# Experts: the order of all engines' steps given as a list, in place of a greedy planner

## The chip, the cores and the metric

The kernel runs on one core of a Trainium2 chip. The metric is the device time of one execution in microseconds. Five engines take their instructions in order, each from its own stream, and wait for each other through semaphores: TensorE (PE, with weight loads as PEld), VectorE (DVE), ScalarE (ACT), GpSimd (POOL) and SyncE (SP, which issues DMAs). The three timed runs of the kernel before took 904.2, 904.42 and 906.09 us.

## The reference

Attention comes first: 8 batches, 8 heads, 576 tokens of 64 numbers each, causal softmax joined with a linear memory `M_prev` by a gate from `beta`. Its output, 4608 tokens of 512 numbers, goes to 8 experts:

```python
logits = x @ w_gate                       # 4608 x 8
order = np.argsort(-logits.flatten())     # token-expert pairs, best first
# a token takes the first expert that still has room (576 tokens each)
h = np.maximum(x[mask] @ w1[e], 0.0)      # 512 -> 1024
out[mask] = h @ w2[e]                     # 1024 -> 512
```

The sort is never made. Expert by expert, the kernel finds the logit at which the fullest expert reaches 576 tokens, assigns these tokens, takes them out and goes on.

## The kernel before, in words

The attention part (lines up to 1413) and its own planner's numbers (`PR`) are the same before and after. The change is in the experts' part, `moe_all`, and it concerns order alone.

`moe_all` builds a list of steps. `SC.add(name, [(engine, duration)], function, r=, w=, after=, acq=, rel=, prio=)` adds one; `r` and `w` name what it reads and writes, from which its predecessors follow; `acq` and `rel` take and free a buffer of a pool (`pr` 2, `ph` 2, `py` 2 banks of PSUM, `ys` 3, `wst` 4 in SBUF). `SC.run` (line 763) then orders all steps: it goes through planned time, and for each engine takes, of the steps that could start within `tol` of the earliest, the one with the smallest `prio`. `prio` comes from `PM`, a table of offsets by kind of step and by expert. The durations in the code are the planner's. At last `for x in ...: x.fn(x)` issues each step's instructions in that order, so that the list is the order on every engine. Semaphores are set by the framework from what instructions really read and write; a wrong belief of the planner costs time, not correctness.

For each of eight experts (n = 0 to 7) there are these groups of steps:

- **Routing** (n < 7): six DVE steps prepare the logits, PE turns them, DVE copies them to `LwT`. Twelve rounds of bisection follow. In a round ACT (`sign`, L1656) and DVE (two counts, L1658) count how many logits pass three thresholds; DVE prepares the next base (`bs`, L1659); a matmul (L1417 `pr<-c,blk`) sums the counts over partitions; DVE compares (`kk`, L1664) and sets the next threshold (`th`, L1665). Then come `lo`, `hi`, the choice of the expert, ties and its tokens.
- **Lists**: prefix sums and comparisons (`triF`, `X`, `se`, `sa`, `oh`, counts, `ids`) give the 576 token numbers in five pieces. POOL gathers each (L1496), and the tokens are turned by a DMA, for n = 0 by PE (L1533) with copies by DVE and ACT (L1538, L1539).
- **Weights**: SP reads the expert's number into a register and issues four loads of 1 MB into `wst` (k = 0, 1 are w1, 2, 3 are w2). Each is split into two float16 parts in two halves: ACT scales in place (L1572) and copies to `wh` (L1573), POOL subtracts to `wl` (L1574, step `sp`, numbered 0 to 7). For the first two halves of n = 0 ACT does both (L1569) and DVE subtracts (L1570, `sv`).
- **FFN** (PE, two products of 192 and 112 matmuls, L1417): first product, for each of 8 f, 12 pairs of matmuls into `ph` and `prem`; ACT takes ReLU (`hh`, L1616), DVE the low part (`hl`, L1617), which frees `ph`. Second product, row tiles i = 0, 4, 1, 2, 3 of 24 or 16 matmuls into `py`; ACT takes it to `ys` (L1631; for i = 4 with DVE, L1633 and L1634), POOL scatters it (L1636). For n = 0 the first two f run tile by tile (`first`), as the tokens arrive.

While PE is in the FFN of expert n, DVE, ACT and POOL route expert n + 2 at most, gather its tokens and split its weights, and the routing matmuls of twelve rounds stand between those of the FFN.

The staging buffer `wst` was freed for the planner with the second half's subtraction (`rel=[('wst',B)] if h==1`).

Of the kernel before, what the change touches and what calls it, by code (L numbers as in the profile page):

```python
# [722 lines left out]
PM = {'T0': -3424.04,  # L723
 'TE': -702.39,
 'dl': {'0': {'gather': -1836.58, 'hh': -28.8, 'hl': 3481.83, 'list': 2655.0, 'moe': -21.88, 'route': -449.74, 'scat': 628.6, 'split': 797.73, 'turn': 806.47, 'wload': -1061.14},
        '1': {'gather': -2182.93, 'hh': -561.25, 'hl': -507.97, 'list': 738.65, 'moe': -816.64, 'route': 1812.2, 'scat': 1447.48, 'split': -1917.9, 'turn': 1120.92, 'wload': 569.59},
        '2': {'gather': 803.19, 'hh': -3791.98, 'hl': -2517.75, 'list': 4060.27, 'moe': -2830.38, 'route': 1411.82, 'scat': -257.8, 'split': -767.47, 'turn': -699.12, 'wload': -520.47},
        '3': {'gather': 783.42, 'hh': 752.55, 'hl': -4377.08, 'list': 117.47, 'moe': 2959.38, 'route': 123.24, 'scat': 1084.4, 'split': -825.2, 'turn': 559.13, 'wload': -4384.5},
        '4': {'gather': 645.39, 'hh': 463.84, 'hl': -2065.23, 'list': 314.59, 'moe': -2361.69, 'route': 677.63, 'scat': -3330.92, 'split': 4348.68, 'turn': 4693.11, 'wload': 723.19},
        '5': {'gather': 1141.95, 'hh': -1781.07, 'hl': -1655.72, 'list': 1577.46, 'moe': -593.59, 'route': 1224.57, 'scat': 232.55, 'split': 2059.93, 'turn': 2978.05, 'wload': 2114.96},  # L730
        '6': {'gather': -1842.39, 'hh': -359.44, 'hl': 2014.66, 'list': -966.97, 'moe': -1531.6, 'route': -1010.83, 'scat': 39.14, 'split': -3339.22, 'turn': -4662.8, 'wload': -443.47},
        '7': {'gather': -755.49, 'hh': 1071.48, 'hl': -182.98, 'list': 1302.37, 'moe': 2877.95, 'route': -1338.67, 'scat': -1147.04, 'split': 1130.89, 'turn': 1140.99, 'wload': 1242.07}},
 'off': {'gather': -603.49, 'hh': -1284.7, 'hl': -3245.18, 'list': -2019.85, 'moe': 3320.21, 'route': -4237.96, 'scat': -1349.2, 'split': 1057.19, 'turn': -14.46, 'wload': 519.8},
 'ph': 2000.0,
 'run': {'tol': 26.8},
 's0': 2}
# [7 lines left out]
class Sched:  # L744
# [18 lines left out]
    def run(self,tol=100,sem=170,same=110,t0=0.0,hwg=450,dlat=1300,dend=950,ph=2800.0,thr=3060,pel=60):  # L763
# [650 lines left out]
def moe_all(ctx,tc,Lw,cst,xd,w1,w2,out):  # L1414
# [3 lines left out]
    P_=PM  # L1418
# [33 lines left out]
    def pr(nm,n,x=0.0):  # L1452
        return P_['T0']+P_['TE']*n+P_['off'].get(nm,0.0)+x+DL.get(str(n),{}).get(nm,0.0)
# [24 lines left out]
    def lists(n):  # L1478
# [49 lines left out]
        if n==0:  # L1528
            for i in range(5):
# [5 lines left out]
                a=SC.add('turn',[('T',430)],f,r=[('xg',i)],acq=(pn,),prio=pr('turn',0),wg=1024)  # L1535
# [10 lines left out]
    def weights(n,ks=(0,1,2,3)):  # L1546
# [4 lines left out]
        for k in ks:  # L1551
# [11 lines left out]
            fl=lambda t: t.rearrange('p a b -> p (a b)')  # L1563
            for h in range(2):
                s=slice(2*h,2*h+2); ws=lambda B=B,s=s: wst[B.buf['wst']][:,s]
                pc=k*2+h; key=('w',n%2,k,h)
                rel=[('wst',B)] if h==1 else ()
                if n==0 and pc<P_.get('s0',4) or [n,pc] in P_.get('sv',[]):
                    a=SC.add('sa1',[('A',947)],lambda x,ws=ws,k=k,s=s: A_.activation(wh[:,k,s],ws(),AF.Copy,scale=64.0),w=[key+('h',)],after=[ld],prio=pr('split',n,.5*pc))  # L1569
                    SC.add('sv',[('V',1135)],lambda x,ws=ws,k=k,s=s: V_.scalar_tensor_tensor(fl(wl[:,k,s]),fl(ws()),64.0,fl(wh[:,k,s]),op0=ALU.mult,op1=ALU.subtract),r=[key+('h',)],w=[key+('l',)],after=[ld],rel=rel,prio=pr('split',n,.5*pc))  # L1570
                else:
                    a=SC.add('sa2',[('A',947)],lambda x,ws=ws: A_.activation(ws(),ws(),AF.Copy,scale=64.0),after=[ld],prio=pr('split',n,.5*pc))  # L1572
                    b=SC.add('sa3',[('A',947)],lambda x,ws=ws,k=k,s=s: A_.copy(wh[:,k,s],ws()),w=[key+('h',)],after=[a],prio=pr('split',n,.5*pc))  # L1573
                    SC.add('sp',[('P',2079)],lambda x,ws=ws,k=k,s=s: G_.tensor_sub(wl[:,k,s],ws(),wh[:,k,s]),r=[key+('h',)],w=[key+('l',)],after=[b],rel=rel,prio=pr('split',n,.5*pc))  # L1574
# [4 lines left out]
    def ffn(n):  # L1579
# [23 lines left out]
        for f in range(8):  # L1603
# [16 lines left out]
        for i in (0,4,1,2,3):  # L1620
# [15 lines left out]
            SC.add('scat',[('P',1250 if i<4 else 1200,'p',0,(1250,'n'))],lambda x,e=e,i=i,r_=r_: G_.indirect_dma_start(out=outv[5*n+i],out_offset=bass.IndirectOffsetOnAxis(ap=idx[0:r_,i:i+1],axis=0),in_=yss[e.buf['ys']][0:r_],in_offset=None),r=[('idx',n%3,i)],after=[e],rel=[('ys',e)],prio=pr('scat',n,pos[0]))  # L1636
    for n in range(8):
        if n<7:
# [14 lines left out]
            for r in range(NR):  # L1653
                i=r%2; t_,b_,c_=th[i],bs[i],cc[i]; x0=rp['x']
                for j in range(KV,K_):
                    SC.add('sign',[('A',547)],lambda x,j=j,t_=t_,c_=c_: A_.activation(scs[j-KV],LwT,AF.Sign,bias=t_[:,4:5],accum_out=c_[:,j:j+1]),r=['LwT',('th',i)],w=[('c',i,j)],prio=pr('route',n,rp['x']))  # L1656
# [72 lines left out]
    for x in SC.run(ph=P_.get('ph',5000.0),**P_.get('run',{})): x.fn(x)  # L1729
# [45 lines left out]
```

## Time and profile before

| | us |
|---|---|
| median of three timed runs | 904.42 |
| the profiled execution | 910.64 |
| its span, first to last instruction | 908.8 |
| PE busy | 803.3 (88%) |
| DVE busy | 670.7 (74%) |
| ACT busy | 580.7 (64%) |
| POOL busy | 543.7 (60%) |

The profile is of one execution. A matmul's end is modelled, so the busy time of PE is more than its work; from start to start is the better measure of it. Times on POOL are rough. A row of the timeline gives the start, the length, engine, line, operation, output and inputs, and in brackets how long the engine was idle before and what ended that. All times are from the span's start. Attention lasts until about 434 us, then PE waits for the routing of expert 0; its first FFN matmul is at 484.4 us and the last one of expert 7 at about 899.4.

### The profile page before, as it was taken

To read this page: it belongs to the slowest core of one execution; us is meant where nothing else is said; L and a number is where in the kernel's file an instruction comes from. 1 tells how busy PE (TensorE), PEld (TensorE's weight loads), DVE (VectorE), ACT (ScalarE), POOL (GpSimd) and SP (SyncE) were. 2 spreads that over 40 slices of the span, in tenths; PEclk is the share of its full clock that TensorE was granted. 3 is DMA by queue.
4 is the path that set the end of the run, shared out by engine and by line. 5 is a ranking of instruction groups with operands and counts; after the bars stand their busy time and mean duration, and the time that the engine had idled before them with its cause. 6 is when DMAs were issued, how large, how long until landed. Compare 5 with 4: busy or idle time off the path is not lost.

```text
span 908.8 us, 24389 instructions
## 1 busy us (share of the span) xinstructions
PE 803.3 (88%) x9240; PEld 526.2 (58%) x9240; DVE 670.7 (74%) x2507; ACT 580.7 (64%) x1027; POOL 543.7 (60%) x564
## 2 busy tenths in 40 slices
PE   3687998999999899999226999999999999999995
PEld 2475887777787688888115445454444444444442
DVE  8798898999999899997788878787867774111020
ACT  4767787887898888976226674848383846552120
POOL 5776886887898786866104492928174646852101
PEclk9999899999999999999557999999999999999998
DMA  5566777765757566334124455566463828940001
GB/s 127 117 142 132 166 155 156 165 149 127 161 130 168 120 139 136 86 71 92 48 93 146 164 144 195 143 213 148 167 168 124 226 89 208 248 150 18 35 13 41
DMA packets 231755, 120.86 MB, mean 133 GB/s; under 512 B 199509, under 2 KB 208725, under 8 KB 231637
## 3 DMA queue, kind: packets, MB, share of 16 engines
q1 hardware_dynamic: 225749, 100.42, 45.2%
q0 software_dynamic: 5888, 18.88, 6.7%
q8 instruction: 72, 1.18, 0.5%
q14 instruction: 46, 0.38, 0.1%
HBM read 72.40 MB, written 18.87 MB: 100 GB/s over the span
## 4 chain that ended last, share of the span: by engine, by line
PE 49%; DVE 22%; issue 12%; DMA 6%; POOL 5%; ACT 3%; SPq 2%; another core or an unknown queue 0%; POOLq 0%; DVEq 0%; ACTq 0%
PE py L1417 15%; PE ph L1417 15%; PE pb L892 7%; PE avo L892 5%; DVE pb L1067 4%; DVE scr L1658 2%; DVE xt L1264 2%; DMA xT<-xs 2%; PE pb L1052 2%; PE prem L1417 2%; DVE pl L1210 2%; SPq L959 1%; POOL h L1043 1%; PE pr L1417 1%; DMA qM<-qT 1%
## 5 line engine op out<-in xcount | busy, mean ns | idle before, releaser
L1574 POOL TENSOR_TENSOR wl<-wst,wh 128x1024 f16<-128x1024 f32 x62 | 131.3, 2140 | 80.8 <-ACT wh L1573 59.5
L1417 PE MATMUL ph<-xT,wh 128*128 128x512 f16 (+1 forms) x560 | 162.9, 364 | 2.8 <-DVE hl L1617 1.4
L1067 DVE CUSTOM_DVE_ANT_0 pb<-pb,maskF 128x128 f32<-128x128 f32 (+3 forms) x256 | 124.7, 497 | 7.4 <-PE pb L892 3.7
L892 PE MATMUL pb<-qT,kT 128*128 128x64 f16 (+3 forms) x576 | 106.1, 245 | 8.2 <-DVE mx L1067 1.8
L1636 POOL DMA_INDIRECT out_dram<-ys,idx x40 | 38.9, 973 | 119.1 <-ACT ys L1631 99.8
L1205 ACT ACTIVATE ph<-pb 128x512 f16<-128x512 f32 x144 | 86.0, 597 | 29.1 <-PE pb L892 23.0
L1617 DVE SCALAR_TENSOR_TENSOR hl<-ph,hh 128x512 f16<-128x512 f32 x64 | 44.0, 688 | 80.2 <-ACT hh L1616 77.2
L1417 PEld LDWEIGHTS <-wh 128*128 128x128 f16 x1072 | 68.4, 98 | 59.6 <-issue 3.5
L892 PE MATMUL pb<-qM,kB 128*128 128x64 f16 (+3 forms) x576 | 99.2, 244 | 1.7 <-DMA qM<-mr 1.7
L1417 PE MATMUL py<-wh,hh 128*128 128x512 f16 x256 | 97.0, 379 | 1.5 <-ACT hh L1616 1.1
L1417 PE MATMUL ph<-xT,wl 128*128 128x512 f16 (+1 forms) x280 | 97.7, 363 | 0.0
L1417 PE MATMUL py<-wl,hh 128*128 128x512 f16 x256 | 97.0, 379 | 0.0
L1417 PE MATMUL prem<-xT,wh 128*128 128x64 f16 x512 | 96.3, 193 | 0.0
L1658 DVE TENSOR_SCALAR_CACHE_REDUCE scr<-p_LwT,th 128x320 f16<-128x320 f32 x168 | 85.1, 543 | 2.7
L1616 ACT ACTIVATE hh<-ph 128x512 f16<-128x512 f32 x64 | 38.0, 593 | 76.2 <-PE ph L1417 55.5
L892 PE MATMUL pb<-kT,qM 128*128 128x512 f16 (+5 forms) x384 | 77.6, 314 | 8.8 <-DVE mx L1067 3.4
L1417 PEld LDWEIGHTS <-hh 128*128 128x128 f16 x512 | 47.3, 97 | 56.2 <-ACT hh L1616 1.3
L1656 ACT ACTIVATE scs<-p_LwT,th 128x320 f16<-128x320 f32 x84 | 47.0, 560 | 50.7 <-DVE th L1665 40.2
L892 PE MATMUL avo<-V,ph 128*128 128x65 f16 x1344 | 78.7, 194 | 0.0
L892 PE MATMUL avo<-V,pl 128*128 128x65 f16 x672 | 74.9, 196 | 0.0
L892 PEld LDWEIGHTS <-ph 128*128 128x128 f16 x1344 | 70.6, 98 | 5.1 <-issue 0.9
L1496 POOL DMA_INDIRECT xg<-xd,idx x40 | 38.6, 964 | 51.6 <-DVE sa L1517 35.0
(304 smaller groups left out, 2358.3 us busy)
## 6 DMA issues: line engine op xcount, KB each, us to landing
wst<-in_moe_w_dram SPq DMA_DIRECT2D x32, 1024.0 KB, 7.7
kf<-in_k_dram SPq DMA_DIRECT2D x64, 128.0 KB, 2.8
qf<-in_q_dram SPq DMA_DIRECT2D x64, 128.0 KB, 2.8
xd<-xs SPq DMA_DIRECT2D x16, 512.0 KB, 3.5
vf<-in_v_dram SPq DMA_DIRECT2D x48, 128.0 KB, 2.8
kB<-kT SPq DMA_DIRECT2D x15, 288.0 KB, 3.4
qM<-qT SPq DMA_DIRECT2D x15, 288.0 KB, 5.5
vF<-in_v_dram SPq DMA_DIRECT2D x16, 128.0 KB, 3.1
```

What stands on the lines that cost most here:

```text
L892: def MM(*a,**kw): mm(*a,skip_group_check=True,**kw)
L1052: for i in range(a,b_): nc.tensor.transpose(p[:,128*(i-a):128*(i-a)+128],g()[:,i],cst['idh'])
L1067: Q=lambda o,i,n: nc.vector.tensor_tensor_reduce(out=i,in0=i,in1=cst['maskF'][:,512-n:512],scale=1.0,scalar=-3e38,op0=ALU.add,op1=ALU.max, ...
L1205: c=SC.add('Eh',[('A',478)],lambda x,a=a: nc.scalar.activation(phs_[x.buf['ph']][:,0:512],pbb[a.buf['pb']],AF.Exp,scale=0.125),acq=('ph',) ...
L1417: def MM(*a,**kw): mm(*a,skip_group_check=True,**kw)
L1496: SC.add('gather',[('P',1250 if i<4 else 1200,'p',0,(1250,'n'))],lambda x: G_.indirect_dma_start(out=xg[0:r_,i],out_offset=None,in_=xd,in_ ...
L1574: SC.add('sp',[('P',2079)],lambda x,ws=ws,k=k,s=s: G_.tensor_sub(wl[:,k,s],ws(),wh[:,k,s]),r=[key+('h',)],w=[key+('l',)],after=[b],rel=rel ...
L1616: b=SC.add('hh',[('A',478)],lambda x,a0=a0,f=f: A_.activation(hh[:,f],phb[a0.buf['ph']],AF.Relu),w=[('hh',f)],after=[y],prio=pr('hh',n,pos ...
L1617: SC.add('hl',[('V',602)],lambda x,a0=a0,f=f: V_.scalar_tensor_tensor(hl[:,f],phb[a0.buf['ph']],0.0,hh[:,f],op0=ALU.max,op1=ALU.subtract), ...
L1636: SC.add('scat',[('P',1250 if i<4 else 1200,'p',0,(1250,'n'))],lambda x,e=e,i=i,r_=r_: G_.indirect_dma_start(out=outv[5*n+i],out_offset=ba ...
L1656: SC.add('sign',[('A',547)],lambda x,j=j,t_=t_,c_=c_: A_.activation(scs[j-KV],LwT,AF.Sign,bias=t_[:,4:5],accum_out=c_[:,j:j+1]),r=['LwT',( ...
L1658: V(462,lambda x,j=j,t_=t_,c_=c_: V_.tensor_scalar(scr[j],LwT,t_[:,j+1:j+2],0.0,op0=ALU.is_ge,op1=ALU.add,accum_out=c_[:,j:j+1]),r=['LwT', ...
```

## The change

`SC.run` gets an argument: with `order` it doesn't plan but calls the new `given`, which walks a list of step numbers, checks that each step's predecessors are ahead of it, and hands out the buffers that a third string names. `PM` loses its offsets. Many durations change, which now order nothing. A new step `wrel` of no engine frees `wst` after both halves' last readers.

```diff
-PM = {'T0': -3424.04, ... 'run': {'tol': 26.8}, 's0': 2}
+PM = {'T0': -3424.04, 'TE': -702.39, 'dl': {}, 'off': {}, 'ph': 2000.0, 's0': 2}
+PM_ORDER = ('''
+0 1 2 3 4 5 8 7 9 6 11 12 10 13 16 14 15 17 18 19 20 23 21 22 25 26 24 27 29 28 ...
+''','''
+
+''','''
+010101010021103010100111200011310210011010013020100112001102011301200110011100120 ...
+''')
...
+    def given(self,ids,alts,bufs):
+        al,bu=[iter(''.join(x.split())) for x in (alts,bufs)]; free={k:set(range(v)) for k,v in self.pools.items()}; out=[]
+        for i in map(int,ids.split()):
+            x=self.n[i]; a=x.alts[int(next(al)) if len(x.alts)>1 else 0]; x.eng=a[0]; x.var=a[2] if len(a)>2 else None
+            assert all(d.start is not None for d in x.deps)
+            for p in x.acq: x.buf[p]=int(next(bu)); free[p].remove(x.buf[p])
+            for p,o in x.rel: free[p].add(o.buf[p])
+            x.start=len(out); out.append(x)
+        assert len(out)==len(self.n)
+        return out
+    def run(self,order=None,tol=100,...):
+        if order: return self.given(*order)
...
# gather 1250 or 1200 -> 965 or 930; turn 430 -> 600; sp 2079 -> 2100; M 243 -> 245;
# hh 478 -> 490; scat 1250 or 1200 -> 980 or 905; sign 547 -> 465
...
-                rel=[('wst',B)] if h==1 else ()
+                both.append(z)
+            SC.add('wrel',[('Z',0)],lambda x: None,after=both,rel=[('wst',B)],prio=0)
...
-    for x in SC.run(ph=P_.get('ph',5000.0),**P_.get('run',{})): x.fn(x)
+    for x in SC.run(PM_ORDER): x.fn(x)
```

A number in the list is the place of a step in the order in which the code adds them. Read so, the list has these orders, among 3150 steps:

- DVE, expert 0's rounds: in rounds 0, 2, 3, 4, 5, 9 `kk`, `bs`, `th`, in the others `bs`, `kk`, `th`.
- DVE at the start of the first FFN: ... round 1's counts (of expert 1), `bs`, first split `sv.0`, `kk`, `th`, round 2's `bs`, first tile copy, round 2's counts, second tile copy, `kk`, second split `sv.1`, `th`, third tile copy.
- PE at the end of the first pass: tile 4 of f = 0 (8 steps), 2 steps of f = 1, round 5's matmul, 2 steps, round 6's matmul, 4 steps, f = 2. DVE there: round 5's `kk`, `th`, round 6's counts, `hl` of f = 0, `kk`.
- ACT at the end of expert 0's first product: `hh` of f = 4, 5, 6, a scaling of expert 1's weights, `hh` of f = 7, a scaling, the ReLU of the last 64 tokens, two copies to `wh`.
- PE between two rounds in a second product: mostly 10 matmuls.
- POOL, expert 2: `sp.3`, `sp.1`, five gathers, `sp.4`, a scatter of expert 1, `sp.2`, a scatter, `sp.5`, two scatters, `sp.0`, `sp.7`, `sp.6`. Expert 1: `sp.2`, four gathers, a scatter of expert 0, a gather, `sp.4`, `sp.1`, `sp.0`.

## Rows read from the trace of the kernel before

**Rows 1.** Busy time by stretch: length, then PE, PEld, DVE, ACT, POOL, PEclk, DMA.
```profile
484.40:516.20 31.80, 29.00 (x305) 19.31 (x305) 26.24 (x127) 19.68 (x41) 12.08 (x6) 0.93 0.32 109
...
544.40:595.40 51.00, 51.00 (x345) 24.95 (x344) 41.33 (x185) 32.19 (x60) 28.06 (x20) 1.00 0.57 168
595.40:647.50 52.10, 51.64 (x346) 24.96 (x345) 40.31 (x181) 31.69 (x59) 27.52 (x19) 1.00 0.54 157
647.50:700.60 53.10, 51.88 (x347) 24.93 (x346) 40.37 (x194) 30.34 (x54) 26.61 (x18) 1.00 0.54 157
700.60:754.60 54.00, 52.50 (x354) 24.88 (x353) 41.06 (x193) 33.99 (x58) 26.98 (x18) 1.00 0.64 195
```
**Rows 2.** TensorE's waits, 485 to 909: who for whom, total us, times, longest.
```profile
PE pr L1417 <- DVE scr L1658: 3.0, 5, 1.5
PE pr L1417 <- DVE pl L1659: 1.6, 1, 1.6
PE ph L1417 <- DVE hl L1617: 1.4, 2, 0.9
```
**Rows 3.** Timelines of ACT and PE, end of expert 0's first product: start, length.
```profile
516.69 2.00 ACT L1572 ACTIVATE wst<-wst 128x1024 f32<-128x1024 f32 x2 [3.94 <-DMA wst<-in_moe_w_dram]
...
520.48 0.59 ACT L1616 ACTIVATE hh<-ph 128x512 f16<-128x512 f32 x1
...
521.12 0.39 PE L1417 MATMUL py<-wh,hh 128*128 128x512 f16 x1 [1.08 <-ACT hh L1616]
```
**Rows 4.** Timelines of PE, DVE, POOL: a usual round, one within the gathers.
```profile
445.29 0.19 PE L1417 MATMUL pr<-c,blk 128*128 128x3 f16 x1 [1.58 <-DVE scr L1658]
445.51 0.16 DVE L1664 SCALAR_TENSOR_TENSOR kk<-pr,need 128x3 f32<-128x3 f32 x1
...
668.41 0.17 PE L1417 MATMUL pr<-c,blk 128*128 128x3 f16 x1
...
668.77 0.90 POOL L1496 DMA_INDIRECT xg<-xd,idx  x1 [0.31 <-issue]
...
670.90 0.16 DVE L1664 SCALAR_TENSOR_TENSOR kk<-pr,need 128x3 f32<-128x3 f32 x1 [3.12 <-PE ph L1417]
```
**Rows 5.** Timelines of DVE and PE, start of expert 0's FFN.
```profile
482.65 1.22 DVE L1570 SCALAR_TENSOR_TENSOR wl<-wst,wh 128x1024 f16<-128x1024 f32 x1
...
483.92 0.42 DVE L1538 COPY xT<-py 128x512 f16<-128x512 f16 x1
...
484.39 0.37 PE L1417 MATMUL ph<-xT,wh 128*128 128x128 f16 x2 [1.24 <-DVE xT L1538]
```
**Rows 6.** Timelines of DVE and PE, end of expert 0's first pass.
```profile
495.94 0.68 DVE L1617 SCALAR_TENSOR_TENSOR hl<-ph,hh 128x512 f16<-128x512 f32 x1
...
496.67 0.38 PE L1417 MATMUL ph<-xT,wh 128*128 128x512 f16 x1 [0.46 <-DVE hl L1617]
```
**Rows 7.** Busy time by stretch, where the granted clock rises.
```profile
485.30:488.70 3.40, 3.38 (x34) 3.38 (x35) 3.07 (x16) 2.15 (x6) 2.64 (x2) 0.50 0.01 2
488.70:492.10 3.40, 3.40 (x65) 3.40 (x63) 2.90 (x14) 1.93 (x6) 0.00 (x0) 1.00 0.65 233
```
**Rows 8.** Timeline of PE, ties of expert 1.
```profile
512.28 0.17 PE L1417 MATMUL pr<-blk,c 128*128 128x8 f16 x1
...
513.04 0.18 PE L1417 MATMUL pr<-tie,tri 128*128 128x40 f16 x1
```
**Rows 9.** Timeline of POOL: gathers and splits.
```profile
525.43 0.95 POOL L1496 DMA_INDIRECT xg<-xd,idx  x1 [0.30 <-issue]
526.68 0.94 POOL L1496 DMA_INDIRECT xg<-xd,idx  x1 [0.30 <-issue]
...
530.09 6.30 POOL L1574 TENSOR_TENSOR wl<-wst,wh 128x1024 f16<-128x1024 f32 x3
```
**Rows 10.** Timeline of ACT: a sign and what follows it.
```profile
505.69 0.56 ACT L1656 ACTIVATE scs<-p_LwT,th 128x320 f16<-128x320 f32 x1
...
506.26 0.57 ACT L1616 ACTIVATE hh<-ph 128x512 f16<-128x512 f32 x1
```

More of the change, by code (lines that the diff above doesn't have):

```diff
@@ L721 @@
         'L': {'pet': 1}}}
[L723 to L736, printed above, removed]
+PM = {'T0': -3424.04, 'TE': -702.39, 'dl': {}, 'off': {}, 'ph': 2000.0, 's0': 2}
+PM_ORDER = ('''
[78 rows of a table added]
+''')
 class Node:
@@ L762, in add, with run @@
         self.n.append(x); return x
-    def run(self,tol=100,sem=170,same=110,t0=0.0,hwg=450,dlat=1300,dend=950,ph=2800.0,thr=3060,pel=60):
+    def given(self,ids,alts,bufs):
[8 more added lines that the diff above has]
+        return out
+    def run(self,order=None,tol=100,sem=170,same=110,t0=0.0,hwg=450,dlat=1300,dend=950,ph=2800.0,thr=3060,pel=60):
+        if order: return self.given(*order)
         N=len(self.n)
@@ L1495, in gather @@
             r_=64 if i==4 else 128
-            SC.add('gather',[('P',1250 if i<4 else 1200,'p',0,(1250,'n'))],lambda x: G_.indirect_dma_start(out=xg[0:r_,i],out_offset=None,in_=xd,in_offset=bass.IndirectOffsetOnAxis(ap=idx[0:r_,i:i+1],axis=0)),r=[('idx',i3,i)],w=[('xg',i)],prio=pr('gather',n))
+            SC.add('gather',[('P',965 if i<4 else 930,'p',0,(965,'n'))],lambda x: G_.indirect_dma_start(out=xg[0:r_,i],out_offset=None,in_=xd,in_offset=bass.IndirectOffsetOnAxis(ap=idx[0:r_,i:i+1],axis=0)),r=[('idx',i3,i)],w=[('xg',i)],prio=pr('gather',n))
         allx=[('idx',i3,i) for i in range(5)]
@@ L1534, in lists @@
                 pn='py'
-                a=SC.add('turn',[('T',430)],f,r=[('xg',i)],acq=(pn,),prio=pr('turn',0),wg=1024)
+                a=SC.add('turn',[('T',600)],f,r=[('xg',i)],acq=(pn,),prio=pr('turn',0),wg=1024)
                 def ev(x,i=i,a=a,pn=pn,h=0):
@@ L1562, in weights @@
             chain('wst',ld)
-            fl=lambda t: t.rearrange('p a b -> p (a b)')
+            fl=lambda t: t.rearrange('p a b -> p (a b)'); both=[]
             for h in range(2):
@@ L1573, in weights @@
                     b=SC.add('sa3',[('A',947)],lambda x,ws=ws,k=k,s=s: A_.copy(wh[:,k,s],ws()),w=[key+('h',)],after=[a],prio=pr('split',n,.5*pc))
-                    SC.add('sp',[('P',2079)],lambda x,ws=ws,k=k,s=s: G_.tensor_sub(wl[:,k,s],ws(),wh[:,k,s]),r=[key+('h',)],w=[key+('l',)],after=[b],rel=rel,prio=pr('split',n,.5*pc))
+                    z=SC.add('sp',[('P',2100)],lambda x,ws=ws,k=k,s=s: G_.tensor_sub(wl[:,k,s],ws(),wh[:,k,s]),r=[key+('h',)],w=[key+('l',)],after=[b],prio=pr('split',n,.5*pc))
+                both.append(z)
+            SC.add('wrel',[('Z',0)],lambda x: None,after=both,rel=[('wst',B)],prio=0)
     last={}
@@ L1655, in moe_all @@
                 for j in range(KV,K_):
-                    SC.add('sign',[('A',547)],lambda x,j=j,t_=t_,c_=c_: A_.activation(scs[j-KV],LwT,AF.Sign,bias=t_[:,4:5],accum_out=c_[:,j:j+1]),r=['LwT',('th',i)],w=[('c',i,j)],prio=pr('route',n,rp['x']))
+                    SC.add('sign',[('A',465)],lambda x,j=j,t_=t_,c_=c_: A_.activation(scs[j-KV],LwT,AF.Sign,bias=t_[:,4:5],accum_out=c_[:,j:j+1]),r=['LwT',('th',i)],w=[('c',i,j)],prio=pr('route',n,rp['x']))
                 for j in range(KV):
```

8 lines of the change are left out of this document (4 added, 4 removed), and 76 rows, old and new, of the table PM_ORDER.

## The prediction

> **What bounds the kernel now.** I read four views in this order: busy time by stretch, TensorE's waits, the timelines of the engines around each of those waits, and DVE against PE around the gathers. The stretches [rows 1] cut the second half of the span at the first matmul of each expert. From 484.4 to 899.6 PE is the bound: in the stretch of expert 1 it is busy 51.00 of 51.00 us. In the stretches of experts 2, 3 and 4 it does the same work in 52.1, 53.1 and 54.0 us. Ahead of 484.4 the chain of routing rounds on DVE is the bound, and no order of steps can shorten a chain in which each link needs the one before. So the reader is to see that an order can win only what PE waits for after 484.4. The three largest rows of the waits [rows 2] add to 6.0 us: five matmuls of a routing round (L1417, pr) waited for DVE's counts, one of them waited 1.6 us, and two matmuls of a first product (ph) waited for `hl`. The next-largest, 1.08 us, is the second product waiting for `hh` on ACT [rows 3].
>
> **What the change does to each.** I numbered the steps in the order in which the code adds them (3150, as many as the list has) and read the list as an order for each engine. No instruction is added or removed: the freed staging buffer is a step of no engine, and the durations in the code are no longer used to order anything. The sum is therefore one of waits that go and waits that come. It is made against the profiled execution, 910.64 us (span 908.8 and 1.84 around it), which lies 6.22 over the median of 904.42.
>
> *Rounds of expert 0.* In six of twelve rounds (0, 2, 3, 4, 5, 9) `bs` (L1659) comes behind `kk` (L1664), where before it always stood ahead, in the time that DVE waits for the matmul. The trace shows 0.28 us from `kk` to `th`; with `bs` between them, which can start 0.09 us after `kk` and takes 0.25 from start to start, `th` starts at 0.34 [rows 4]. That is +0.06 six times, +0.4 us; two instructions (L1475, L1476) move behind the first counts, -0.2. Together +0.2; bounds 0 and +0.8 (0.13, `bs`'s issue time, six times).
>
> *Start of the first expert.* Before, two splits (L1570) of 1.22 us each stand ahead of the first copy of a turned tile (L1538), and PE starts 0.47 us after that copy's start [rows 5]. In the list one split stands ahead, and the threshold of the next round (0.25 more): the copy comes 0.9 us earlier, less the 0.2 above. The second split comes two copies and two counts later, so the low part of the first pass waits for it, about half a microsecond. The gathers don't move: the third and last of them start where they did, since the five that POOL issues are 1.25 us apart. What remains by the end of the first pass is 0.3 us of lead. I take -0.3.
>
> *First pass to second pass.* Before, PE stood from 494.3 to 496.67, since the third ph tile needs `hl`, which stood behind a round's two counts [rows 6]. In the list two rounds' matmuls (5 and 6) stand in the last columns of the pass and `hl` again behind round 6's counts: from the matmul of round 5, 0.22 to `kk`, 0.28 to `th`, 0.25 to the first count, 0.94 for two counts, 0.60 for `hl`, 0.15 to PE, 2.4 us. The stall is re-formed, not removed; -0.3 as one `hh` is no longer behind a scaling on ACT. Together with the start: -0.6, bounds -1.6 (the whole 0.9 stays and `hl` is ready on time) and +1.7, the clock. The granted clock was 0.50 until 488.7 and 1.00 from there, after 3.4 us in which PE was busy 3.38 [rows 7]. In the list the half-microsecond hole falls into that stretch. Were the clock to rise 3.4 us later, work of 1.7 us at full speed would cost 3.4.
>
> *Second product of expert 0.* `hh` of the last f waited on ACT behind two scalings and two copies of expert 1's weights, which began when their load had come, at 516.69, and PE waited 1.08 us, 1.3 more between two starts than elsewhere [rows 3]. In the list only one scaling (0.95) stands ahead: `hh` ends 1.0 + 0.6 us after the load, at about 518.3, and PE wants it at 519.5. The wait goes: -1.3. If the load came 1.2 us later, the wait would be back; bounds -1.3 and 0.
>
> *Ties of expert 1.* The routing matmuls at 512.28 and 513.04 each hold PE for about 0.3 us, waiting for DVE [rows 8]; the list leaves 10 pairs and 4 pairs of matmuls between them, and DVE's work there takes as long: -0.3, bounds -0.6 and +0.3.
>
> *Experts 2 to 4.* Their 1.1 + 2.1 + 3.0 = 6.2 us over expert 1's stretch [rows 1] are the largest sum in sight, and I count nothing of it. In each, a round's matmul ends and DVE's `kk` doesn't start: 2.49 us from start to start instead of 0.22, while the last gather is issued and lands (the longest of four such cases, beside a usual one) [rows 4]. The other three, of 1.2 to 2.1 us, also lie within the gathers, and the matmuls run on meanwhile. Only afterwards PE waits, for the late round. Two things speak against counting this as a gain. The list keeps five gathers a round trip from the same rounds. And the span of this one execution is 4.4 us over the median of those without a profile: I put most of the late starts down to the taking of the profile, since the other waits, above, follow from the order of the steps and can't be that. The Trainium skill, in "Runtime: NRT & Kernel Launch", section "The ~15µs preamble/postamble breakdown", says that a profile's total is about 6.2 us over the reported time through work after the kernel. That would put our 6.22 outside the span and leave the late starts real; but the span alone, first instruction to last, is over the median here, so it can't be all. It raises rival 1 a little.
>
> *POOL.* New waits come from here. Expert 2's first split half (`sp.0`) stands late on POOL: from `sp.3` to its own end there are 6 splits and 9 indirect DMAs. A split takes 2.10 and an indirect DMA 1.25 from start to start [rows 9], 12.6 + 11.25 = 23.9 us. They can start some 27 us after expert 1's first matmul (the turn of the logits stands in the list behind 82 pairs, 20 us by the diff's 0.245 a pair, 1.3 of routing between them, then 5.5 for `LwT`, a sign, a scaling and a copy), and end at 50.9; PE asks for it at 51.0, the stretch of expert 1, and 0.5. I take 0; bounds 0, since nothing waited there before, and +2.4 (rival 2). Expert 1's has 1.7 us to spare by the same sum, its turned tiles 2.5; those of experts 3 to 7 stand early in the list.
>
> Sum: +0.2 is in the -0.6; -0.6 - 1.3 - 0.3 = **-2.2 us**, 908.4 for a profiled execution and **902.2 us** without.
>
> **Rivals.**
> 1. *The waits around the gathers are in every execution, and the list's wider spacing takes them.* Then 2.2 + 6.2 = 8.4 us go: 896.0. For it: the list puts 10 matmuls, 2.2 us, between two rounds where there were 9; and experts 2 to 4 really differ. Against: 2.2 us don't hide a start that is 2.5 late, and the 4.4 us above.
> 2. *POOL becomes the bound of a first pass.* The list's order was made with 0.965 and 0.98 us for an indirect DMA (the new numbers of the diff) where the trace has 1.25 from start to start [rows 9], and with 0.465 for a sign that takes ACT 0.57 [rows 10]. Ten DMAs and twelve signs an expert are 2.9 + 1.2 = 4.1 us more than planned; less the 1.7 to spare, 2.4 us at the start of experts 1 and 2 each: 902.2 + 4.8 = 907.0. It decides from the point at which `sp.0` ends after PE's last second product. For it: splits and DMAs are packed without gaps there. Against: my walk, with 1.25, still just fits. The Trainium skill, in "Perfetto Trace Analysis", section "GPSIMD Engine Instruction", tells to time POOL by the spacing of starts and not by the reported length, which is what the diff's numbers look like; our rows agree with it (0.95 reported, 1.25 spacing).
> 3. *Nothing comes of it.* Each wait removed is re-formed a few steps later, since the routing chain of the next expert (twelve rounds and the lists) keeps DVE busy 41 of 51 us [rows 1]: 904.4. For it: the 2.4 us at the end of the first pass is re-formed in my own walk. Against: the `hh` wait has no successor there.
>
> **How the numbers follow.** Forecast 0.50, rival 1 0.15, rival 2 0.17, rival 3 0.18. 0.2% is 1.8 us, about what a measurement of this kernel can tell from no change. Around the forecast I see 900.5 to 904.0; some six tenths of that case lie below 902.6, so faster is 0.30 + 0.15 + 0.03 = 0.48; of rival 2 three quarters are above 906.2, and a little of the others: slower 0.17; the same 0.35. The range runs from 897.5, which leaves out most of rival 1, to 906.5, which leaves out half of rival 2: about 0.2 outside.
>
> **What would show it.** Right: `hh` ends before PE asks, no wait for ACT in the second product of expert 0; the third ph tile still waits about 2 us; `kk` again starts 1 to 2.5 us late where gathers land, and stretches of 52 to 54 us stay in the profile. Wrong: first matmuls of experts 1 or 2 that wait for POOL's split (rival 2); stretches of experts 2 to 4 all at 51 and a median under 898 (rival 1); a clock that rises at 492 instead of 488.7; a load of expert 1's weights that lands a microsecond later on PE's time.

## The result, and the profile after

The changed kernel takes 913.41 us (median of five runs, 912.55 to 918.37), the kernel before 906.09 (five runs): ratio 1.0097, 95% interval 1.0072 to 1.0121. It is slower by 7.3 us, where 2.2 us less had been forecast. The profiled execution took 918.37 us, with a span of 916.6.

The stretches of the changed kernel, by first and second product for expert 0 (length, PE, PEld, DVE, ACT, POOL, PEclk, DMA); they answer to [rows 1]:

```profile
484.40:516.10 31.70, 28.63 (x307) 18.45 (x306) 27.32 (x126) 20.13 (x42) 13.49 (x6) 0.97 0.34 123
516.10:544.70 28.60, 26.30 (x140) 11.71 (x139) 21.96 (x96) 23.66 (x41) 18.79 (x14) 1.00 0.73 206
544.70:599.80 55.10, 52.79 (x344) 25.18 (x345) 44.80 (x186) 31.48 (x57) 30.22 (x21) 0.97 0.52 149
599.80:651.20 51.40, 51.40 (x346) 25.10 (x345) 39.86 (x182) 31.08 (x56) 29.73 (x20) 1.00 0.56 154
651.20:702.90 51.70, 51.32 (x346) 24.99 (x345) 38.69 (x176) 30.52 (x54) 25.63 (x17) 1.00 0.51 149
702.90:753.40 50.50, 50.50 (x339) 24.64 (x338) 35.81 (x158) 30.50 (x54) 27.49 (x19) 1.00 0.54 161
...
804.30:859.50 55.20, 50.73 (x306) 24.06 (x305) 6.72 (x10) 13.79 (x20) 22.00 (x16) 0.94 0.26 63
```

Expert 1 takes 55.1 us instead of 51.0, and expert 6 takes 55.2 instead of 47.7, though no routing goes on beside it. PE's waits from 485 to 916 (who for whom, total, times, longest), which answer to [rows 2]:

```profile
PE ph L1498 <- DVE hl L1699: 4.7, 2, 4.5
PE pr L1498 <- DVE scr L1740: 4.0, 3, 2.3
PE ph L1498 <- DMA xT<-xg: 2.3, 1, 2.3
```

Three of these waits are new: the 4.5 us, the 2.3 us for DMA, and one of the 2.3 us for `scr`. Their timelines (start, length; in brackets the idle time before and its end):

```profile
526.20 0.16 DVE L1574 SCALAR_TENSOR_TENSOR idx<-pl,pp 128x5 int32<-128x5 f32 x1
...
532.13 0.93 POOL L1718 DMA_INDIRECT out_dram<-ys,idx  x1 [0.30 <-DVE scr L1740]
533.37 0.96 POOL L1577 DMA_INDIRECT xg<-xd,idx  x1 [0.30 <-issue]
...
544.68 0.39 PE L1498 MATMUL ph<-xT,wh 128*128 128x512 f16 x1 [2.29 <-DMA xT<-xg]
...
570.94 4.26 POOL L1654 TENSOR_TENSOR wl<-wst,wh 128x1024 f16<-128x1024 f32 x2 [18.21 <-ACT wh L1653]
...
571.08 2.05 DVE L1785 TENSOR_TENSOR need<-need,cl 128x1 f32<-128x1 f32 x1
573.16 2.05 DVE L1786 SCALAR_TENSOR_TENSOR need<-a,need,b 128x3 f32<-128x3 f32 x1
...
577.41 0.18 PE L1498 MATMUL pr<-c,blk 128*128 128x3 f16 x1 [2.31 <-DVE scr L1740]
...
797.14 0.96 POOL L1577 DMA_INDIRECT xg<-xd,idx  x1 [3.89 <-DMA xT<-xg]
...
804.98 0.94 POOL L1718 DMA_INDIRECT out_dram<-ys,idx  x1 [0.17 <-issue]
...
809.99 0.60 ACT L1713 ACTIVATE ys<-py 128x512 f32<-128x512 f32 x1 [6.18 <-DMA out_dram<-ys,idx]
...
814.83 0.58 PE L1498 MATMUL ph<-xT,wh 128*128 128x512 f16 x1 [4.46 <-DVE hl L1699]
```

- **A, 542.0 to 544.7.** Expert 1's token numbers come at 526.20 on DVE (523.25 before), since the list sets the second matmul of its list behind the turn of the next logits and two counts behind two others. A scatter among the five gathers adds 1.25. The second product of expert 0 now ends 2 us earlier, and PE waits 2.29 us for the turned tiles.
- **B, 574.7 to 577.4.** Two tiny instructions of DVE's step `need` take 2.05 us each; six other times they take 0.16 and 0.22. Each ends with one of the two splits that POOL started at 570.94 (2.13 us each). A round of routing comes 3.7 us late.
- **C, 810.2 to 814.8.** The second scatter of expert 5 stands on POOL behind gathers of expert 7, which wait for expert 6's tiles to be turned (797.14). Until it has landed, ACT can't refill its `ys` buffer (809.99), and the `hh` of expert 6 stand behind that on ACT: PE waits 4.46 us for `ph` to come free.

Around both the granted clock falls to the lower of its two levels: from 578.3 to 581.7 behind B, and from 813.8, 1.0 us before PE starts again, to 820.6 around the end of C. The 5.7 us at 0.50 with PE at work cost 2.9:

```profile
814.80:820.50 5.70, 5.67 (x24) 2.32 (x24) 0.57 (x1) 1.62 (x2) 5.52 (x4) 0.50 0.17 64
```

### The profile page after: what moved, and what is told of

Its sections match the earlier page's. It is cut to its first block, busy times and chain, and to the rows that moved or that the text cites. A ratio compares the mean times of both kernels' runs of the same rounds, so it can differ in the third digit from the quotient of the medians.

```text
span 916.6 us, 24330 instructions
## 1 busy us (share of the span) xinstructions
PE 807.4 (88%) x9240; PEld 528.3 (58%) x9240; DVE 676.8 (74%) x2507; ACT 581.7 (63%) x1027; POOL 546.5 (60%) x564
## 4 chain that ended last, share of the span: by engine, by line
PE 43%; DVE 22%; issue 13%; DMA 8%; POOL 7%; ACT 3%; SPq 2%; POOLq 0%; DVEq 0%; ACTq 0%
PE ph L1498 14%; PE py L1498 12%; PE pb L973 6%; DVE pb L1148 5%; PE avo L973 5%; DVE xt L1345 2%; DMA xT<-xs 2%; DVE pl L1291 2%; PE pb L1133 2%; DVE scr L1740 2%; PE prem L1498 2%; DMA xT<-xg 2%; POOL h L1124 1%; DMA qM<-qT 1%; POOL out_dram L1718 1%
## 5 line engine op out<-in xcount | busy, mean ns | idle before, releaser
L1498 PE MATMUL ph<-xT,wh 128*128 128x512 f16 (+1 forms) x560 | 165.1, 366 | 7.4 <-DVE hl L1699 4.7
L1286 ACT ACTIVATE ph<-pb 128x512 f16<-128x512 f32 x144 | 86.0, 597 | 31.8 <-PE pb L973 22.0
L1652 ACT ACTIVATE wst<-wst 128x1024 f32<-128x1024 f32 x62 | 64.3, 1049 | 15.9 <-DMA wst<-in_moe_w_dram 15.9
```

Source lines behind the costliest of these rows:

```text
L1286: c=SC.add('Eh',[('A',478)],lambda x,a=a: nc.scalar.activation(phs_[x.buf['ph']][:,0:512],pbb[a.buf['pb']],AF.Exp,scale=0.125),acq=('ph',) ...
L1498: def MM(*a,**kw): mm(*a,skip_group_check=True,**kw)
```

## The experiments

Each edit is a list of moves: a step is put right before ("b") or after ("a") another, and the walk applies them to the recorded list.

```diff
+        ids=list(map(int,ids.split())); bufs={i:[int(next(bu)) for p in self.n[i].acq] for i in ids}
+        for i,w,j in MOVES: ids.remove(i); ids.insert(ids.index(j)+(w=='a'),i)
```

The five jobs fell on five chips, and the traces are of two kinds. "Late signals" are completions of PE, DVE or ACT whose semaphore update is recorded over 0.25 us after the instruction's end, of some 3,500 in a trace. The trace behind [rows 1] to [rows 10] is of the kind with them, the changed kernel's first is not.

| job: before, us | kernel | us | ratio (95%) | late signals |
|---|---|---|---|---|
| first: 906.09 | changed | 913.41 | 1.0097 (1.0072-1.0121) | 0 (before: 61) |
| 1: 914.95 | e1 scatter moved | 916.32 | 1.0021 (0.9990-1.0052) | 64 |
| | e2 list moved | 918.85 | 1.0050 (1.0019-1.0081) | 61 |
| | e3 need moved | 911.65 | 0.9974 (0.9940-1.0009) | 64 |
| | e4 all three | 912.74 | 0.9985 (0.9957-1.0013) | 69 |
| 2: 915.99 | e5 changed | 917.26 | 1.0015 (0.9977-1.0053) | 59 |
| | e6 one input | 916.19 | 1.0003 (0.9975-1.0031) | 63 |
| | e7 plain gathers | 909.39 (one run) | - | 12 |
| | e8 all three, one input | 916.48 | 1.0011 (0.9978-1.0043) | 63 |
| 3: 906.09 | e9 before | 907.0 (one run) | - | 0 |
| | e10 before, plain gathers | 907.80 | 1.0024 (0.9999-1.0049) | 1 |
| | e11 changed, plain gathers | 908.26 | 1.0033 (1.0010-1.0055) | 0 |
| | e12 scatter later | 920.92 (one run) | - | 1 |
| 4: 909.37 | e13 changed | 919.21 | 1.0090 (1.0056-1.0125) | 62 |
| | e14 = e8 | 911.19 | 1.0026 (1.0004-1.0047) | 70 |
| | e15 = e1 | 915.07 | 1.0052 (1.0025-1.0080) | 67 |
| | e16 = e3 | 916.88 | 1.0072 (1.0044-1.0101) | 64 |
| 5: 905.63 | e17 = e8 | 907.25 | 1.0019 (0.9997-1.0041) | 0 |
| | e18 a round later | 908.37 | 1.0021 (1.0007-1.0036) | 1 |

**Wait C: e1, e12, e15.**

```diff
# e1, e15
+MOVES = [(2386, 'b', 2907)]  # n5.scat4 before n7.gather1
# e12
+MOVES = [(2386, 'a', 2867)]  # n5.scat4 behind n7.sp.1
```

e1: 

> The changed order, with one step moved: the second scatter of expert 5 (row tile 4) stands ahead of the first gather for expert 7 on POOL instead of five steps behind it. Theory (queue): that scatter, due at 793, waited on POOL behind three gathers, which waited for the turned tiles of expert 6, and two splits; until it had landed (809.9) ACT could not refill its ys buffer, and the two hh of expert 6 stood behind that on ACT. The wait of 4.66 us at 810.2 goes, and with it the 5.7 us at clock 0.50 behind it (2.9 us): 7.3 us less, 913.4 -> about 906, ratio to the kernel before 1.000. Rival (transfers): the slow turns of tokens (6.0 us each beside the weight loads) are the cause, so that hh or the first matmuls of expert 6 wait for something else: less than 2 us go, ratio 1.006 or more.

e12: 

> The changed order with the second scatter of expert 5 two steps later still on POOL, behind one more gather and one more split (3.4 us). Theory (queue): the last ys of expert 5 on ACT waits for that scatter to land, the first two hh of expert 6 stand behind it, and PE waits before the third f of expert 6's first product: about 3.7 us there, with some 3 us more at half clock, as in the changed kernel's first trace (4.66 and 2.9). Rival (that wait came from the slow turns of tokens): no wait over 1 us there.

e15: 

> Only the second scatter of expert 5 moved ahead of the gathers of expert 7. Without late signals, theory: the wait of expert 6 and the half clock behind it are gone, up to 7 us less than the changed kernel of this job and no less than 2 (it is not in each execution); trace with the other two waits as before. Rival: no difference.

e1 didn't decide. On its chip PE idles only 0.45 and 0.24 us there in e2 and e3, which lack the move; in e1 the wait is gone. In e12 the cause is made worse, and the wait comes (4.62 us; about 3.7 were expected), by the same chain of scatter, `ys`, `hh`, with the clock at 0.50 from 815.9 to 822.7:

```profile
808.96 0.93 POOL L1721 DMA_INDIRECT out_dram<-ys,idx  x1 [0.17 <-issue]
...
812.95 0.60 ACT L1716 ACTIVATE ys<-py 128x512 f32<-128x512 f32 x1 [6.07 <-DMA out_dram<-ys,idx]
...
817.78 0.58 PE L1501 MATMUL ph<-xT,wh 128*128 128x512 f16 x1 [4.62 <-DVE hl L1702]
```

In job 4 e15 is 4.1 us under the changed kernel, but the two intervals overlap; its trace lacks the wait, which is 0.80 us in e13. The length of expert 6's stretch decides: 55.1 us in the changed kernel's first trace and 54.9 in e12, 47.7 or 47.8 in the seven traces with the scatter moved ahead, e17 among them, on a chip without late signals:

```profile
801.20:848.90 47.70, 47.70 (x306) 23.08 (x305) 6.81 (x10) 14.52 (x21) 19.16 (x13) 1.00 0.30 70
```

But in the six other traces with that scatter and the POOL gathers at their places in the list (e2, e3, e5, e6, e13, e16, all on chips with late signals) expert 6 takes only 48.0 to 48.7. So the queue makes the wait possible, and two transfers decide its size. In the changed kernel's first trace the gathers ahead waited 3.89 us for turned tiles and the scatter started 0.7 us behind expert 6's first matmul, landing 5.0 us later; in e3 they waited 1.84, it started 1.4 ahead, and landed in 2.8. The 2.0 and 2.2 us come to the difference between the waits of 4.46 and 0.24. The rival, slow turns, is thus half of it. Why the transfers differ isn't shown.

**Wait B: e3, e6, e16.**

```diff
# e3, e16
+MOVES = [(1018, 'b', 1029)]  # n2.need before n2.list.cnt012
# e6
-V_.tensor_tensor(need,need,cl,op=ALU.add)
-V_.scalar_tensor_tensor(need3,cst['a3'],need,cst['b3'],op0=ALU.mult,op1=ALU.add)
+V_.tensor_scalar(need,need,cl,None,op0=ALU.add)
+V_.tensor_scalar(need3,cst['a3'],need,None,op0=ALU.mult)
+V_.tensor_scalar(need3[:,KV:K_],need3[:,KV:K_],-5120.0,None,op0=ALU.add)
```

e3: 

> The changed order, with one DVE step of expert 2 (need, five instructions) moved ahead of three counts, 1.2 us earlier. Theory (port): two of its instructions with two SBUF inputs, of 128x1 and 128x3 elements, took 2.05 us each because each began while POOL ran a split of 2.13 us, and ended with it; moved ahead they run before the splits begin and take 0.16 and 0.22 us. The wait of 2.69 us at 574.7 and the half clock of about 4 us behind it go: 4.1 us, 913.4 -> 909.3, ratio 1.0035. Rival (these two instructions wait for something of their own, such as their code or their operand): they take 2.05 us at the new place too and nothing goes, ratio 1.008; whichever instruction of DVE then runs beside the splits stays at its usual length.

e6: 

> The changed order untouched; in DVE's step need the two instructions with two SBUF inputs are written as three with one SBUF input each (cl as a scalar per partition, the constants as immediates), at the same place on DVE, with the same result. Theory (port): beside POOL's split they take 0.1 to 0.2 us each instead of 2.05, and the wait of 2.7 us with the half clock behind it goes: 4 to 4.7 us less than the changed kernel of the same job, ratio 0.999 to 1.005. Rival (the two waited for something that belongs to this place, such as code or operands): the three take about 4 us together as well, ratio as the changed kernel.

e16: 

> Only DVE's need moved ahead of three counts. Theory, on any chip: the wait of 2.69 us in expert 1's second product and the half clock behind it are gone, 4 to 4.7 us less than the changed kernel of this job (on the first chip it was run on it stood 4.7 below a version with the wait). Rival: no difference.

Moved ahead of the splits, the same two instructions are short again (e16):

```profile
571.13 0.16 DVE L1788 TENSOR_TENSOR need<-need,cl 128x1 f32<-128x1 f32 x1
571.32 0.22 DVE L1789 SCALAR_TENSOR_TENSOR need<-a,need,b 128x3 f32<-128x3 f32 x1
```

e3 takes 4.7 us less than e1, as expected (4.1). e16 takes 2.3 less than e13, which is within the noise of these two. The traces decide: expert 1's stretch is 54.8 to 55.2 us in the nine with the step unchanged at its place in the list, and 51.5 to 52.4 in the seven with it moved, on chips of both kinds. Of the half clock behind the wait little is left over: the four traces with it have 55.0 to 55.2, the five without 54.8 to 54.9, since there PE waits for the next rounds instead (0.9 us in e5 and e7). Rewritten at their old place (e6), two of the three are short beside the split and one is not:

```profile
574.48 4.26 POOL L1657 TENSOR_TENSOR wl<-wst,wh 128x1024 f16<-128x1024 f32 x2 [19.64 <-ACT wh L1656]
...
574.62 0.21 DVE L1788 TENSOR_SCALAR need<-need,cl 128x1 f32<-128x1 f32 x1
574.87 1.81 DVE L1789 TENSOR_SCALAR need<-a,need 128x3 f32<-128x3 f32 x1
576.71 0.15 DVE L1789 TENSOR_SCALAR need<-need 128x1 f32<-128x1 f32 x1
```

So neither code nor operands of the place hold them, but the split; and one SBUF input is not always enough. e6 stands 1.1 us below e5, where 4 were expected, and that is within the noise; its stretch of expert 1 is 53.0 us. The Trainium skill, in "SBUF — State Buffer", section "SBUF: two separate sides", says that a DVE instruction with two SBUF inputs, or in a mode that uses both ports, and a GpSimd instruction that reads SBUF shut each other out for a whole instruction. The rows agree, with one exception: `cpen<-ohe,cpen`, two inputs, began 0.02 to 0.03 us after the split's recorded start in ten traces and took its usual 0.16. Whether the 1.81 us with one input is such a mode no run shows.

**Wait A: e2, and all together: e4, e8, e14.**

```diff
# e2
+MOVES = [(634, 'b', 887), (635, 'b', 888), (636, 'b', 888), (594, 'a', 638), (406, 'a', 638)]
# n1.list.g2 before n2.turnlog; cnt34, ids before n2.LwT; n1.sp.2, n0.scat4 behind n1.gather1
# e4: these and the moves of e1 and e3; e8, e14, e17: e4 and the rewriting of e6
```

e2: 

> The changed order, with expert 1's list finished earlier: the second matmul of its list stands ahead of the turn of the logits, its last two counts and token numbers ahead of LwT, and on POOL a split and a scatter of expert 0 behind the five gathers instead of among them. Theory: the first matmul of expert 1 waited 2.46 us for turned tokens that came 4.25 us later than before (token numbers 3.0 later, one scatter of 1.25 between the gathers); it goes: 913.4 -> about 911, ratio 1.0055. The wait for DVE at 574.7 stays, unless the steps shift against each other and the collision of DVE and POOL there breaks up: then 4 us more go, ratio 1.001. Rival (a weight split is what is late at that place): no change, ratio 1.008.

e4: 

> The three edits together. Theory (three separate waits, and the changed order is else as good as its matmuls are dense): 2.5 + 4.1 + 7.3 = 13.9 us go: 913.4 -> 899.5, ratio 0.993, faster than both kernels. Rival (each wait comes back a few steps later, since routing is the bound): 906 or more, ratio 1.000.

e8: 

> All three moves (list of expert 1 earlier and its gathers together, need ahead of three counts, second scatter of expert 5 ahead of the gathers of expert 7) and need with one SBUF input per instruction. Theory: none of the three waits is in its trace, and what is left are late signals beside the gathers: 1.0 to 1.5 % less than the changed kernel of this job, ratio to the kernel before 0.990 to 0.998. Rival (the moves only shift the waits): ratio 1.000 or more.

e14: 

> The three moves and need with one SBUF input each. Without late signals, theory: all three waits gone, 12 to 14 us less than the changed kernel of this job, 898 to 902, ratio to the kernel before 0.991 to 0.996. With late signals: within 0.3 % of the kernel before. Rival (the waits only shift): within 3 us of the changed kernel.

e2 says nothing of the price: on its chip PE stands 2.5 to 3.0 us before a round in the second product of expert 0 (below), and the tiles are in time in e1 and e3 too. The wait is there without the edit in e5 (0.4 us), e12 (2.4), e15 (0.5) and e16 (2.6), and in none of the traces with it. Without late signals the second product takes 28.6 and 28.7 us with the wait (the first trace, e12), 26.4 and 26.5 with the edit (e17, e18). The expectations of e4 and e8 fell: in jobs 1 and 2 the mended versions stand within 0.2% of the kernel before, and so does the changed kernel in e5 (expected: 1.004 or more), with only wait B and 0.4 us of A in its trace. In job 4, where the changed kernel loses 0.90%, e14 takes back 8.0 of its 9.8 us, clear of noise, and stands within 0.3% of the kernel before, as expected for a chip with late signals.

**Late signals: e5, e7, e9, e10, e11, e13.** e7, e10 and e11 leave out the choice of rows: for experts 1 to 7 they bring rows 0 to 575.

```diff
# e7, e11 in the changed kernel, e10 in the kernel before
-lambda x: G_.indirect_dma_start(out=xg[0:r_,i], ...
+(lambda x: nc.sync.dma_start(out=xg[0:r_,i],in_=xd[128*i:128*i+r_])) if n else lambda x: G_.indirect_dma_start(...
```

e5: 

> The changed kernel itself once more, beside the kernel before on the same chip, for a second trace. Theory (three waits, of which two hang on a microsecond of lead): the wait of DVE's need behind POOL's splits comes again at the same place (2.05 us twice, PE waits 2.7 and loses 2 more at half clock), since nothing ahead of it varies; the wait of 4.66 us in expert 6 and the one of 2.67 us at expert 1's first product come or go with a microsecond of a transfer. Ratio 1.004 to 1.010. Rival (the first result was that chip's): ratio within 0.998 and 1.002.

e7: 

> The changed order; for experts 1 to 7 the gathers are plain DMAs of the same size from SP that bring rows 0 to 575 instead of the expert's tokens, so the output of these experts is left wrong. In five of six traces so far some 60 completions of PE, DVE and ACT were signalled 0.25 to 4.5 us late, all within 4 us of an indirect DMA on POOL. Theory (POOL's issue of indirect DMAs holds up the other engines' signals): in the stretches of the gathers of experts 1 to 7 no late signal is left; those beside scatters stay. Rival (the traffic of the rows, or the taking of the profile): about as many as in the changed kernel's trace of the same job.

e9: 

> The kernel before once more, for a trace. On this kind of chip it took 915 to 916 us, where the three runs shown with it took 904 to 906. Theory (late signals cost the order before more than the changed one): its trace has some 60 late signals beside indirect DMAs, and waits of PE for rounds of routing beside gathers add to 8 us or more, against 5.7 us (2.9, 0.5 and 2.3) in the changed kernel's second trace. Rival (the chip is slower throughout): first matmul of the experts and the dense stretches later or longer by the same share, the waits as in the first trace (6 us).

e10: 

> The order before; gathers of experts 1 to 7 as plain DMAs from SP of rows 0 to 575, which leaves the output of these experts wrong. Theory: without late signals beside gathers the order before loses nothing there: 904 to 906 us, ratio 0.987 to 0.990. Rival: ratio 0.995 or more.

e11: 

> The changed order with the same plain gathers (output wrong in the same way). Theory: one run gave 909.4; the wait behind POOL's splits is left (4 us), the wait for expert 1's turned tiles is not (POOL no longer issues its gathers): 908 to 911, ratio 0.992 to 0.996, and 3 to 6 us over the order before with plain gathers, so that the changed order is the slower one as soon as late signals are gone. Rival (the orders differ by nothing but late signals): within 1.5 us of the order before with plain gathers.

e13: 

> The changed kernel beside its mended versions of this job. On a chip without late signals (none in the first trace of the changed kernel, none in four traces of the last chip) theory says 911 to 916, ratio 1.006 to 1.011, with three waits in the trace: 2.7 us at expert 1's first product, 2.69 at a round of expert 1's second product, about 4.7 in expert 6. On a chip with some 60 late signals: ratio 0.999 to 1.004, the second wait only, and 3 and 2 us beside gathers. Rival (the first result was chance): ratio 0.998 to 1.002 on a chip without late signals as well.

In e13 a round's matmul at 537.57, among gathers and a scatter, reaches DVE 3 us late, and PE stands before the next round:

```profile
537.57 0.16 PE L1498 MATMUL pr<-c,blk 128*128 128x3 f16 x1
...
540.59 0.16 DVE L1746 SCALAR_TENSOR_TENSOR kk<-pr,need 128x3 f32<-128x3 f32 x1 [3.44 <-PE py L1498]
...
542.33 0.18 PE L1498 MATMUL pr<-c,blk 128*128 128x3 f16 x1 [2.41 <-DVE scr L1740]
```

e9 met a chip without late signals, so its theory wasn't tried. In it, the order before, the round that was 2.49 us late [rows 4] starts in its usual 0.24, beside the same five gathers:

```profile
668.40 0.17 PE L1417 MATMUL pr<-c,blk 128*128 128x3 f16 x1
...
668.64 0.16 DVE L1664 SCALAR_TENSOR_TENSOR kk<-pr,need 128x3 f32<-128x3 f32 x1 [0.87 <-PE pr L1417]
```

All the late signals of the twelve traces with some 60 of them are of instructions that end within 2 us behind the start of an indirect DMA; there are none elsewhere. With the gathers issued by SP (e7) 12 are left of 59 and no late round. So POOL's issue of indirect DMAs delays them, on some chips and not on others. e10 and e11 were meant to show the orders without them, but the chip of job 3 has none anyway, and plain gathers brought waits of their own, 3.6 us in e10 (until 756.3) and 1.2 in e11: their expectations fell and they decide nothing. That late signals explain why one chip shows 0.97% and another 0.15% fell too: e13 has 62 of them and still 1.0090.

**What the mended order still loses: e17, e18.**

```diff
# e18: the moves of e17 and
+(2499, 'a', 1952)  # n6.r3.mmr behind n4.M2.i0.6
```

e17: 

> The mended version once more, for the other kind of chip. Without late signals, theory (the three waits are all that the changed order loses): 898 to 902, ratio to the kernel before 0.991 to 0.996, a trace without a wait of over 2 us behind 500. With late signals, as the last time: ratio 1.000 to 1.005. Rival (something else is lost as well): ratio over 0.998 without late signals.

e18: 

> The mended version with one matmul of routing (the fourth round of expert 6) placed eight matmuls later on PE, at the end of expert 4's first product, where eight pairs of matmuls stood between it and the round before and PE waited 2.2 us in each trace with late signals. With late signals, theory: the wait shrinks to under 0.7 us and the half clock behind it goes: 2 to 4 us less than the mended version of this job. Without: no difference (within 1 us).

No late signals to speak of came on this chip, so e18's theory wasn't tried. e17's expectation of 898 to 902 fell: its trace has no wait of over 2 us, and it still takes 907.25. Against e9, also without late signals (first product of expert 0, second product, expert 1):

```profile
485.00:517.50 32.50, 29.69 (x306) 19.88 (x306) 26.27 (x127) 19.63 (x41) 12.11 (x6) 0.91 0.31 108
517.50:545.20 27.70, 26.22 (x139) 11.86 (x138) 20.70 (x90) 22.81 (x37) 22.53 (x14) 1.00 0.70 198
545.20:596.10 50.90, 50.90 (x344) 24.91 (x343) 41.12 (x185) 32.10 (x59) 28.31 (x20) 1.00 0.56 169
```

stands e17:

```profile
483.40:517.90 34.50, 31.77 (x307) 20.82 (x306) 27.76 (x127) 20.45 (x42) 13.56 (x6) 0.85 0.33 112
517.90:544.30 26.40, 26.20 (x139) 11.80 (x138) 21.06 (x93) 22.68 (x39) 16.36 (x13) 1.00 0.76 215
544.30:596.70 52.40, 51.30 (x345) 25.04 (x344) 42.87 (x191) 32.60 (x60) 32.54 (x22) 1.00 0.57 161
...
490.40:497.20 6.80, 4.98 (x96) 4.67 (x95) 4.31 (x23) 4.76 (x10) 0.00 (x0) 1.00 0.33 123
497.20:500.60 3.40, 3.40 (x16) 1.46 (x15) 2.00 (x9) 2.91 (x5) 0.31 (x1) 0.50 0.00 0
```

The second product gains 1.3 us, as forecast. The first loses 2.0: the clock rises 7.0 us behind the first matmul instead of 5.8 (0.6 us lost), then in 6.8 us PE was busy only 4.98, with the third `ph` tile's stall at their end, and the next 3.4 us ran at clock 0.50 (1.7 us lost). Such a fall there is in 10 of 17 traces of the changed order and its variants and in none of 3 of the order before, which has that stall too (2.4 us between starts); what sets it off isn't shown. Expert 1 loses 1.5 more, of which PE waits 1.1 on DVE (0.7 for `pl`, 0.4 for `tie`), and experts 2 to 6 together 0.2.

So e17 stands 1.6 us above the kernel before of its job, where the changed kernel stood 7.3 above that of the first, on chips where the kernel before takes the same (905.63 and 906.09).

## Why the prediction was wrong, point by point

**The sum by stretch.** The changed kernel's first trace against e9, both without late signals: first product of expert 0 -0.8, second +0.9, expert 1 +4.2, experts 2 and 3 +0.1, expert 4 -1.8, expert 5 +1.9 (routing moved from one to the other), expert 6 +7.5: +12.0 us. Its first matmul comes 0.6 earlier, which makes the 11.4 between the spans. The timed difference is 7.3. The profiled run is the longest of the five and has the lowest mean clock (0.953 against 0.955 to 0.957), so the others may have had less of wait C; but they have no trace, and the fall in the first product, which this trace lacks, would add some 2 us to any of them.

**Right.** The wait for the last `hh` is gone, and with wait A mended expert 0's second product is 1.3 us shorter in e17 than in e9, the size forecast. The stall before the third `ph` tile is re-formed as worked out, 1.73 and 0.47 us between starts instead of 1.78 and 0.62. Nothing was counted for experts 2 to 4, and nothing came (51.4, 51.7 and 50.5 against 51.4, 51.6 and 52.3 in e9, with 1.9 more in expert 5).

**The step that failed** is the part on POOL, "I take 0". It asked only when the splits come, and three things were not in it:

- Expert 1's tiles, which it gave 2.5 us to spare, came 2.3 late. Nothing in it has the token numbers come later, but the list delays them by 3.0 on DVE and PE; and the 2 us by which the second product ends earlier come off the spare time. In the first trace that eats the 1.3 us won and 0.9 more.
- It looked at each engine's order by itself, and so missed that DVE's `need` now falls beside a split. PE stood 2.3 us, and the seven mends of it shorten expert 1's stretch from 54.8-55.2 to 51.5-52.4. It is in every trace in which the step is unchanged.
- It left experts 3 to 7 out because their splits "stand early in the list". Their scatters don't: one stands behind gathers that themselves wait for tiles, and a `ys` buffer, ACT's queue and PE hang on it. This is the largest term of the first trace, 7.5 us, and 0.3 to 1.0 in six others, all on chips with late signals.

**The rivals.** Rival 2 had the right engine, the right side and nearly the right place, with the wrong link: no split was late at a first matmul, but tiles, a DVE step and a scatter. Rival 1 falls for the chips without late signals. The late starts were put "down to the taking of the profile". A profile alone doesn't make them: e9's trace has none, e13's has 62. Nor do they lengthen profiled executions: in eleven kernels with some 60 of them the profiled one differs from its kernel's median by -4.0 to +4.1 us, -0.1 in the mean. The argument also set a span, 908.8, against a time, which lies some 1.8 above its span in every run, profiled or not; like with like the profiled execution was 6.2 longer.

**The clock, the second step that failed.** The first product was put at -0.6, with +1.7 as a bound. The hole after the second row tile was taken as half a microsecond; PE idles 1.02 us there (until 487.51). In the first trace the clock rose no later for it (486.1, only 1.7 us behind the first matmul; in e9 5.8). That is luck, worth some 2 us by half of the 4.1 us, an estimate; without it the -0.8 would be above nothing. But in eight of the 17 traces of the changed order it rose 7.0 to 7.9 us behind the first matmul, against 4.3 to 5.8 in the three of the order before; these eight and two more have the fall, at 494 to 504. The first product takes 34.2 to 34.9 us in nine traces, 31.6 to 33.0 in eight, and 31.8 to 32.5 in the order before: up to 2.4 us more, over the bound.

**Small things.** The 1.6 us row of [rows 2] is a sixth matmul, which waited for `bs`, not one of the five; nothing rests on it. The tenths put before the first matmul can't be told from chance: it comes at 482.1 to 486.2 in the changed order, at 482.6 to 485.0 in the order before.

**Left open.** Why the changed kernel loses 0.97% and 0.90% on two chips and 0.15% on a third; what sets off the fall in the first product; and whether any mending of this list beats the order before: the best reading, e3, is 0.9974 (0.9940 to 1.0009), and e14 and e17 are above 1.

## What to carry to other kernels

What made this list isn't on record. The planner that it replaces does reckon with such things: in its code a step of DVE marked `slack` is held back behind POOL's work, PE can run at half speed, and an indirect DMA has a time to land. A list fixes what followed from planned times, and the run keeps the order where its times are others; a step that was clear of a split by plan, as `need` is by its mark, may then meet one. That this is how the losses came about is likely, not shown. When you price a new order by hand, follow for each engine not only when its own work ends, but what stands behind each instruction that may wait (a scatter behind a gather, a `ys` behind a scatter, an `hh` behind a `ys`), and write down the spare time of each before you spend the gain. Take a second trace on another chip before you explain waits of a microsecond or two.

## What the runs showed of the hardware

- While POOL issues indirect DMAs, signals of PE, DVE and ACT can be late, by up to 3.5 us where DVE waited for one (e4): about 60 of the 350 to 380 completions within 2 us behind the start of one, on three of the five chips (and in the first trace of the kernel before), 0 or 1 on the other two.
- A DVE instruction of 128x1 or 128x3 elements with two SBUF inputs took 2.05 us beside a POOL split (0.16 and 0.22 away from one), one with a single input of 128x3 took 1.81, and two with a single input of 128x1 took 0.21 and 0.15.
- Behind 2.2 us of stalls in the first product the granted clock was 0.50 for 3.4 us, with PE busy again, in 10 of 17 traces of this order, and stayed at 1.00 in the other 7; around the end of the stall in expert 6 it was 0.50 for 6.8 us (813.8 to 820.6).
- A scatter of 64 rows landed 2.8 us behind its start in one trace (e3) and 5.0 in another (the changed kernel's first).
